# Full-width FFN2 for the first four row tiles of a retention and ELU-MLP kernel, with the second weight matrix loaded by FFN1 tile

## The chip, the cores and the metric

One core of one Trainium2 chip. The metric is device time in microseconds (us) of one execution; a lower number is better. Engines in the profile: PE is TensorE's matmuls, PEld its weight loads, DVE is VectorE, ACT ScalarE, POOL GpSimd, SP SyncE. A "q" after the name is the engine's sequencer, which issues DMAs.

## The reference

```python
# q, k, v: (8, 8, 576, 64), each 0.1 * randn;  w_in: (512, 2048);  w_out: (2048, 512)
scores = q @ k.transpose(0, 1, 3, 2) / sqrt(64)
Dmat   = where(rel >= 0, gamma[h] ** rel, 0)         # rel = query row - key row, causal decay
attn   = (scores * Dmat) @ v                          # (8, 8, 576, 64)
x      = attn.transpose(0, 2, 1, 3).reshape(4608, 512)
h      = x @ w_in                                     # FFN1
g      = where(h > 0, h, exp(min(h, 0)) - 1)          # ELU
out    = g @ w_out                                    # FFN2, (4608, 512) float32
```

## The kernel before

The 4608 rows are 36 units of 128. For each unit: transposes of queries and keys, scores, mask, products, a gating that writes x transposed; then, for groups of units, FFN1 (16 tiles of 128 columns of w_in, each with ELU on ScalarE, GpSimd and VectorE) and FFN2. The order of instructions on every engine is the order of the program. From unit 4 on, everything is interleaved. What concerns us is the start: group 0 is units 0 to 2, group 1 is unit 3; their FFN1 runs while the weights are still coming in, and their FFN2 runs in one piece before the interleaving begins.

```python
def load_w_out(c, f0, f1):                            # by column halves, 256 of 512
    s = (slice(None), slice(f0, f1), slice(c * 256, c * 256 + 256))
    nc.gpsimd.dma_start(w_out_sb[s], w_out_v[s])

def ffn2_cols(u, c0, c1, bank, copy, queue):
    g, it = group_of[u]
    pool, tag = bank
    pm = pool.tile([P, c1 - c0], FP32, name="pmh", tag=tag)
    for ft in range(NFT):                             # 16 matmuls of 256 columns
        nc.tensor.matmul(
            pm, gts[g, ft][:, it * P : (it + 1) * P], w_out_sb[:, ft, c0:c1],
            start=(ft == 0), stop=(ft == NFT - 1),
        )
    ot = opool.tile([P, c1 - c0], FP32, name="oth", tag="ot")
    copy(ot, pm)                                      # VectorE for even u, ScalarE for odd u
    queue.dma_start(out[u * P : (u + 1) * P, c0:c1], ot)
# ...
def load_v(u, after=None, queue=nc.sync):
    vv = raw.tile([P, H, D], FP32, name="rv", tag="rv")
    if after is not None:
        after.memset(vv[0:1, 0, 0:1], 0.0)            # the load waits for this write: a release
    for p0, b, s0, n in place(u):
        queue.dma_start(vv[p0 : p0 + n], v[b, :, s0 : s0 + n, :].rearrange("h p d -> p h d"))
# ... the loads, in this order on GpSimd's queue:
    load_w_in(0)  # after units 1 and 2's queries and keys
    scale_v(0); load_w_in(1); scale_v(1); load_w_in(2)
    load_qk(3); load_v(3, queue=nc.gpsimd); scale_v(2); load_w_in(3)
    load_w_out(0, 0, 16); load_w_out(1, 0, 16)
# ... FFN1 of group 0: tile n needs quarter n // 4 of w_in; unit 3's attention lies within
    for n in range(4, 16):
        f1(0, n, m if n % 4 == 1 else None)
        if n == 9:
            turn(3)
        # ... scale_v(3) in halves at 9 and 10, scores(3) at 11, product(3) at 13
# ... then FFN1 of group 1, and:
    load_qk(4); finish(); load_qk(5); load_v(5, nc.vector); scale_v(4)
    nc.gpsimd.tensor_copy(gx[:, :, S:], gx[:, :, 0:64])
    for u, bank in enumerate((h, h, h, m)):
        ffn2_half(u, 0, bank)                         # all first halves
    load_qk(6); load_v(6, nc.vector); scale_v(5)
    ffn2_half(0, 1, h)                                # second halves between unit 4's attention
    turn(4)
    # ... ffn2_half(1, 1, h), scores(4), ffn2_half(2, 1, h), product(4), turn(5), ffn2_half(3, 1, m)
    f1(2, 0)                                          # FFN1 of unit 4
```

## Time and profile before

| | before |
|---|---|
| time, median of 3 runs | 315.29 us (314.77 to 315.34) |
| span of the profiled run | 313.2 us |
| TensorE busy from 16 to 311 us | 292.73 of 295 us |
| first FFN2 matmul to unit 4's first FFN1 matmul | 32.77 to 49.36, 16.59 us |
| landing of the last quarter of w_in | 25.62 us |
| landing of w_out's two halves | 31.0 and 37.2 us |

TensorE is the bound from 16 us to the end, so a change counts where it alters when TensorE starts, how long its stream is, or where the stream must wait. The lines that show it stand in the prediction. Two reading aids: consecutive matmuls overlap, so their cost is the distance between starts, not their length; and a "landing" here is a DMA's issue plus its time to landing from the DMA view.

### The profile page before, as it was taken

The page shows a single profiled execution, that of the slowest core. Times are in us where ns is not written, and L with a number is a line of the kernel's source. Part 1 is how long each engine was busy: PE and PEld are TensorE (multiplying, and loading weights), DVE is VectorE, ACT ScalarE, POOL GpSimd, SP SyncE. Part 2 cuts the span into 40 slices and gives each one's busy share as a digit, 9 for nine tenths or more (in the row PEclk, how much of TensorE's full clock was granted, in tenths as well). Part 3 has the DMA queues.
Part 4 walks back from the last instruction along what each step waited for, and adds up shares of the span by engine and source line. Part 5 has one row for each costly group of instructions (what it writes and reads, how often), then busy time and mean ns, then how long its engine had stood idle before and what let it go on. Part 6 is the DMA issues. An engine that isn't in the chain of part 4 may idle for free.

```text
span 313.2 us, 7555 instructions
## 1 busy us (share of the span) xinstructions
PE 305.2 (97%) x3028; PEld 173.6 (55%) x3028; DVE 172.5 (55%) x279; ACT 130.8 (42%) x243; POOL 200.2 (64%) x288
## 2 busy tenths in 40 slices
PE   7799999999999999999999999999999999999995
PEld 3477988777765555554554444444444444444444
DVE  4668435756756667655565655565555555434300
ACT  6356215355344543444444443443444344344311
POOL 7977894968977777797777666766664423333300
PEclk9999999999999999999999999999999999999999
DMA  9999999997999999999999999998996200001111
GB/s 156 186 206 199 206 211 177 191 143 75 126 122 178 144 126 195 133 107 198 97 160 134 125 126 132 133 137 128 134 133 86 69 33 36 35 33 39 64 68 68
DMA packets 149219, 39.55 MB, mean 126 GB/s; under 512 B 137600, under 2 KB 145152, under 8 KB 149184
## 3 DMA queue, kind: packets, MB, share of 16 engines
q0 software_dynamic: 79248, 13.64, 56.2%
q1 hardware_dynamic: 67920, 23.14, 39.3%
q10 hardware_dynamic: 2016, 2.29, 2.4%
q8 instruction: 23, 0.38, 0.5%
q14 instruction: 12, 0.10, 0.1%
HBM read 36.70 MB, written 9.44 MB: 147 GB/s over the span
## 4 chain that ended last, share of the span: by engine, by line
PE 88%; DMA 5%; DVE 2%; POOL 2%; SPq 0%; issue 0%; ACT 0%; DVEq 0%; POOLq 0%
PE ph L353 37%; PE pm L378 34%; PE pmh L394 6%; PE sc L212 4%; DMA w_in_sb<-in_moe_w_in_dram 3%; PE o L274 3%; PE st L257 2%; PE o L240 2%; DMA rv<-in_v_dram 2%; PE tr L196 1%; POOL vn L177 1%; DVE pt L224 1%; DVE g L320 1%; POOL qkn L94 1%; POOL w_in_sb L105 0%; DVE xt L287 0%
## 5 line engine op out<-in xcount | busy, mean ns | idle before, releaser
L360 POOL TENSOR_SCALAR m<-e 128x512 bf16<-128x512 f32 (+1 forms) x156 | 90.7, 583 | 95.1 <-ACT e L358 91.5
L353 PE MATMUL ph<-xt,w_in_sb 128*128 128x512 bf16 (+3 forms) x808 | 142.0, 313 | 0.7 <-DVE g L320 0.2
L320 DVE SCALAR_TENSOR_TENSOR g<-ph,m 128x512 bf16<-128x512 f32 (+1 forms) x156 | 99.4, 647 | 76.1 <-POOL m L360 75.3
L358 ACT ACTIVATE e<-ph 128x512 f32<-128x512 f32 (+1 forms) x156 | 87.5, 564 | 124.9 <-PE ph L353 122.1
L378 PE MATMUL pm<-w_out_sb,g 128*128 128x512 bf16 x496 | 125.6, 379 | 0.0
L353 PEld LDWEIGHTS <-w_in_sb 128*128 128x128 bf16 x808 | 68.9, 98 | 53.6 <-DVE g L320 0.9
L378 PEld LDWEIGHTS <-g 128*128 128x128 bf16 x496 | 47.8, 98 | 53.2 <-issue 0.3
L224 DVE TENSOR_TENSOR pt<-sc,mask 128x1024 bf16<-128x1024 f32 (+1 forms) x37 | 44.1, 1193 | 19.7 <-PE sc L212 19.4
L177 POOL TENSOR_TENSOR vn<-rv,gk 128x512 bf16<-128x512 f32 (+1 forms) x37 | 37.8, 1022 | 1.0 <-DMA rv<-in_v_dram 1.0
L94 POOL DMA_DIRECT2D qkn<-in_q_dram x39 | 35.0, 899 | 0.0
L94 POOL DMA_DIRECT2D qkn<-in_k_dram x39 | 33.4, 858 | 0.1
L287 DVE TENSOR_TENSOR xt<-o,gx 128x512 bf16<-128x512 f32 x36 | 24.7, 685 | 14.1 <-PE o L274 13.9
L385 ACT COPY ot<-pm 128x512 f32<-128x512 f32 x31 | 18.1, 585 | 14.5 <-PE pm L378 14.1
L266 ACT CAST sb<-st 128x256 bf16<-128x256 f32 x32 | 11.9, 372 | 19.4 <-PE st L257 16.6
L394 PE MATMUL pmh<-w_out_sb,g 128*128 128x256 bf16 (+1 forms) x176 | 18.3, 263 | 0.0
L394 PEld LDWEIGHTS <-g 128*128 128x128 bf16 x176 | 15.8, 98 | 1.9
L212 PEld LDWEIGHTS <-qkT 64*64 64x64 bf16 x576 | 9.2, 106 | 13.5 <-issue 11.0
L212 PE MATMUL sc<-qkT 64*64 64x128 bf16 x576 | 15.0, 222 | 0.3 <-ACT qkT L198 0.2
L274 PE MATMUL o<-pt,vn 128*64 128x128 bf16 x288 | 14.3, 221 | 0.0
L399 DVE COPY oth<-pmh 128x256 f32<-128x256 f32 (+1 forms) x6 | 2.4, 402 | 18.0 <-PE pmh L394 18.0
L240 PE MATMUL o<-qkT,sb 64*64 64x128 bf16 (+1 forms) x256 | 12.3, 214 | 0.0
L257 PE MATMUL st<-vn,qkn 128*64 128x64 bf16 (+1 forms) x256 | 10.4, 201 | 0.0
(41 smaller groups left out, 89.8 us busy)
## 6 DMA issues: line engine op xcount, KB each, us to landing
rv<-in_v_dram SPq DMA_DIRECT2D x31, 256.0 KB, 5.3
out_dram<-ot SPq DMA_DIRECT2D x27, 256.0 KB, 2.4
qkn<-in_q_dram POOLq DMA_DIRECT2D x31, 128.0 KB, 5.4
qkn<-in_k_dram POOLq DMA_DIRECT2D x31, 128.0 KB, 5.4
w_in_sb<-in_moe_w_in_dram POOLq DMA_DIRECT2D x4, 512.0 KB, 10.0
w_out_sb<-in_moe_w_out_dram POOLq DMA_DIRECT2D x2, 1024.0 KB, 18.0
out_dram<-oth ACTq DMA_DIRECT2D x9, 128.0 KB, 4.7
rv<-in_v_dram SPq DMA_DIRECT2D x8, 128.0 KB, 5.8
```

The lines of the kernel that those rows point to most:

```text
L94: nc.gpsimd.dma_start(kns[u][p0 : p0 + n, c], (q, k)[c][b, :, s0 : s0 + n, :].rearrange("h p d -> p h d"))
L177: nc.gpsimd.tensor_tensor(vns[u][:, h0:h1], raws[u][:, h0:h1], gk[:, u % R, h0:h1].unsqueeze(2).to_broadcast([P, h1 - h0, D]), ALU.mult,)
L212: nc.tensor.matmul(sc[j * 64 : (j + 1) * 64, i, hp], t[r, 1, hp, j * 64 : (j + 1) * 64], t[r, 0, hp], start=(hp == 0), stop=(hp == HP - 1) ...
L224: nc.vector.tensor_tensor(pts[u][:, s].rearrange("p i h t -> p (i h) t"), scs[u][:, s].rearrange("p i h t -> p (i h) t"), m.unsqueeze(1).t ...
L274: nc.tensor.matmul(o[i * D : (i + 1) * D, hp], vns[u][:, h], pts[u][:, i, hp], start=(u % R == 0 and hp == 0), stop=(hp == HP - 1), skip_g ...
L287: nc.vector.tensor_tensor(xts[g][:, :, i * P : (i + 1) * P], os_[u], gx[:, :, s0 : s0 + P], ALU.mult)
L320: nc.vector.scalar_tensor_tensor(gt_, ph, 0.0, m, ALU.max, ALU.min)
L353: nc.tensor.matmul(ph[:, i * n : (i + 1) * n], w_in_sb[:, j, f : f + P], xts[g][:, j, :n], start=(j == 0), stop=(j == KJ - 1), skip_group_ ...
L358: nc.scalar.activation(e[:, w], ph[:, w], AF.Exp)
L360: nc.gpsimd.tensor_scalar(m[:, w], e[:, w], -1.0, 1.0, ALU.add, ALU.mult)
L378: nc.tensor.matmul(pm, gts[g, ft][:, it * P : (it + 1) * P], w_out_sb[:, ft], start=(ft == 0), stop=(ft == NFT - 1))
L394: nc.tensor.matmul(pm, gts[g, ft][:, it * P : (it + 1) * P], w_out_sb[:, ft, c0:c1], start=(ft == 0), stop=(ft == NFT - 1),)
```

## The change

The intent: each FFN2 matmul of the first four units covers all 512 columns, in four banks held open at once, first with FFN1 tiles 0 to 7 of all four units, so that only the first half of w_out's rows is needed at first; hence w_out comes in two parts by FFN1 tile. Unit 3's values leave GpSimd's busy queue.

```diff
-    def load_w_out(c, f0, f1):
-        s = (slice(None), slice(f0, f1), slice(c * 256, c * 256 + 256))
-        nc.gpsimd.dma_start(w_out_sb[s], w_out_v[s])
+    def load_w_out(f0, f1):
+        nc.gpsimd.dma_start(w_out_sb[:, f0:f1], w_out_v[:, f0:f1])
...
-    def ffn2_half(u, c, bank):
-        ffn2_cols(u, c * 256, c * 256 + 256, bank, A if u % 2 else V, nc.scalar)
+    def ffn2_part(u, f0, f1, bank):
+        g, it = group_of[u]
+        if f0 == 0:
+            pool, tag = bank
+            acc[u] = pool.tile([P, DM], FP32, name="pm", tag=tag)
+        for ft in range(f0, f1):
+            nc.tensor.matmul(
+                acc[u], gts[g, ft][:, it * P : (it + 1) * P], w_out_sb[:, ft], start=(ft == 0), stop=(ft == NFT - 1)
+            )
+        if f1 == NFT:
+            ot = opool.tile([P, DM], FP32, name="ot", tag="ot")
+            (A if u % 2 else V)(ot, acc[u])
+            nc.scalar.dma_start(out[u * P : (u + 1) * P, :], ot)
...
     load_qk(3)
-    load_v(3, queue=nc.gpsimd)
     scale_v(2)
     load_w_in(3)
-    load_w_out(0, 0, 16)
-    load_w_out(1, 0, 16)
+    load_w_out(0, 8)
+    load_w_out(8, 16)
...
         product(u)
+        if u == 1:
+            load_v(3, nc.vector)
...
     for u, bank in enumerate((h, h, h, m)):
-        ffn2_half(u, 0, bank)
+        ffn2_part(u, 0, 8, bank)
     load_qk(6)
     load_v(6, nc.vector)
     scale_v(5)
-    ffn2_half(0, 1, h)
+    ffn2_part(0, 8, 16, None)
     turn(4)
... (units 1 to 3 alike)
```

More of the change, by code (lines that the diff above doesn't have):

```diff
@@ L374, in ffn2 @@
             pool, tag = ((ps_o, "o"), (ps_m, "pm"), (ps_h, "ph"))[it] if g == NG - 1 else (ps_m, "pm")
-            acc[0] = pool.tile([P, DM], FP32, name="pm", tag=tag)
-        pm = acc[0]
+            acc["pm"] = pool.tile([P, DM], FP32, name="pm", tag=tag)
+        pm = acc["pm"]
         for ft in range(part * 4, part * 4 + 4):
@@ L503 @@
     load_v(7, nc.vector)
-    ffn2_half(1, 1, h)
+    ffn2_part(1, 8, 16, None)
     scores(4)
@@ L507 @@
     scale_v(6)
-    ffn2_half(2, 1, h)
+    ffn2_part(2, 8, 16, None)
     product(4)
@@ L512 @@
     load_v(8, nc.vector)
-    ffn2_half(3, 1, m)
+    ffn2_part(3, 8, 16, None)
     scores(5)
```

## The prediction

> **What bounds the kernel now.** I read the page's first two parts, then the busy time of the engines by stretch, then the chain that ended last around the changed stage, then the instructions in order of time there, and last the DMA issues one by one.
>
> From the page, parts 1 and 2 and the ends of parts 3 and 5 (busy shares; tenths of busy time in 40 slices of 7.8 us; two groups):
>
> ```profile
> PE 305.2 (97%) x3028; PEld 173.6 (55%) x3028; DVE 172.5 (55%) x279; ACT 130.8 (42%) x243; POOL 200.2 (64%) x288
> ...
> PE   7799999999999999999999999999999999999995
> ...
> PEclk9999999999999999999999999999999999999999
> DMA  9999999997999999999999999998996200001111
> ...
> L378 PE MATMUL pm<-w_out_sb,g 128*128 128x512 bf16 x496 | 125.6, 379 | 0.0
> ...
> L394 PE MATMUL pmh<-w_out_sb,g 128*128 128x256 bf16 (+1 forms) x176 | 18.3, 263 | 0.0
> ```
>
> TensorE is full from slice 3 on, at full clock, and no other engine is above 64%. A mean of 379 ns is the length of one matmul with its drain; it is not what it costs, because 496 of them have a union of only 125.6 us. The cost is the spacing from start to start. The views by stretch confirm the bound (columns: stretch, length, busy, count, clock, DMA share, GB/s; first TensorE alone, then all matmuls of the half-width FFN2 line):
>
> ```profile
> 16.00:311.00 295.00, 292.73 (x2889) 1.00 0.97 124
> ...
> 32.77:41.50 8.73, 8.72 (x80) 7.73 (x80) 1.00 1.60 195
> ```
>
> From 16 to 311 us TensorE lacks 2.3 us of 295. The second line is the changed stage: 80 half-width matmuls in 8.73 us are 109.1 ns each. In full width the same page's rows of four in the chain take 0.86 us, so 0.2157 us each: two halves cost 0.2182, one whole 0.2157.
>
> The chain of waits in order of time from 12 to 52 us (start, length, what):
>
> ```profile
> 12.82 0.89 POOL rv L85
> 13.71 0.98 POOL vn L177
> 14.69 10.93 DMA w_in_sb<-in_moe_w_in_dram
> 25.62 0.05 issue
> 25.67 1.47 PE ph L353 x8
> ...
> 32.94 8.73 PE pmh L394 x80
> 41.67 0.45 PE tr L196 x8
> 42.12 1.75 PE pmh L394 x16
> 43.86 0.35 PE sc L212 x16
> 44.21 1.85 PE pmh L394 x16
> ```
>
> The reader is to see that the chain enters TensorE only once, where the last quarter of w_in lands at 25.62 us, and then stays there. That entry looks like 11 us behind GpSimd's work (unit 3's values issued at 12.82 stand in it), but TensorE had work of its own until 25.6: the start of 25.67 is only some 0.13 us later than the spacing after the scores would have it (spacing between these starts 0.275 us more than the usual one, and 0.145 of that is what every change from scores back to full-array matmuls shows, as at 44.15 and 49.36). So at most 0.13 us hang on that load. Neither half of w_out appears: the first was issued at 15.50 and landed 15.5 us later, at 31.0, used from 32.77; the second issued at 16.64, landing after 20.5 us, at 37.2, used from about 39.75 (32.77 plus 64 times 0.109).
>
> The stage where the tightest hand-over lies, in order of time (start, length, engine, line, count; in brackets idle before):
>
> ```profile
> 41.51 0.61 PE L196 MATMUL tr<-ident,qkn 128*128 128x128 bf16 x8
> 41.71 0.42 DVE L399 COPY oth<-pmh 128x256 f32<-128x256 f32 x1 [3.07 <-PE pmh L394]
> ...
> 42.16 0.42 DVE L197 COPY qkT<-tr 128x512 bf16<-128x512 bf16 x1
> ...
> 42.85 0.58 ACT L198 COPY qkT<-tr 128x512 bf16<-128x512 bf16 x1 [2.52 <-DVE rv L83]
> ...
> 43.80 0.42 PE L212 MATMUL sc<-qkT 64*64 64x128 bf16 x16
> ```
>
> The last piece of unit 4's keys is issued at 36.35 and takes 5.2 us (the DMA view of that moment), so it lands at about 41.5: as the transposes start, whose key half runs 0.22 us in. And ScalarE's copy of the transposed half ends at 43.43, 0.37 us ahead of the scores that read it.
>
> **What the Trainium skill says.** "TensorE: Matmul & The Clock Gate", section Back-to-back issue gap: a warm matmul is spaced N/2.4 + 2.5 ns. The trace agrees: 109.1 against 109.2 for N = 256, 215.7 against 215.8 for N = 512. Halving the number of matmuls saves only the fixed 2.5 ns. Weight loads overlap here (98 ns each, under the 109 ns of a half), so having fewer is worth nothing more.
> "DMA: Bandwidth & Descriptors", section Issuing engines are not separate DMA queues: all queues share the same 16 DMA engines, and another issuer saves only issue time. The trace agrees in that DMA is at 9 tenths throughout this part.
> The same page, section Why small descriptors are slow (HBM only): a fixed cost per packet, worth attention at 256 B or less. The w_out parts go from 1 KB to 2 KB pieces of source (512 B to 1 KB written), so little is to be had: in the stretch 13 to 18 us (w_in, 1 KB pieces written) the core moves 206 GB/s, in 26 to 30 us (w_out, 512 B) 199, 3% less.
>
> **The change part by part.**
> 1. FFN2 at full width: 128 matmuls at 109.1 ns (13.96 us) become 64 at 215.7 (13.81). On the path: -0.16 us.
> 2. Copies out of PSUM: eight of 128x256 (0.42 us on VectorE, 0.37 on ScalarE) become four of 128x512, an estimate of 0.67 and measured 0.585 (the page's 128x512 copy on ScalarE). Less work in total (3.2 to 2.5 us), but each single one is 0.2 us longer, and unit 0's stands ahead of the transposes' copies. Old order: 0.42 copy from 41.71, then qkT on VectorE, then qkT on ScalarE, slack some hundredths to a few tenths. New: the last part ends some 0.1 us earlier, the copy starts at about 41.6 and ends at 42.27, qkT on VectorE ends near 42.7, ScalarE near 43.5; scores want to start at about 43.7. Estimate 0 to +0.15 us, mean +0.05. At unit 2's copy the new end of about 46.75 just meets unit 4's gating at 46.89: 0.
> 3. Banks: all four accumulators stay open from 32.77 to 49. Nobody else takes these banks meanwhile (transposes and scores use another pair, the products two others), and the next FFN1 tiles take those of units 0, 1 and 2, copied out 5 us and more before for the first two and 2 us for the third. The first use of each of the four banks falls where it did (8 times 0.2157 is 1.73 us per unit, 16 times 0.1091 is 1.75). 0.
> 4. w_out by FFN1 tile: the first part is needed at 32.77 as before, the second at 32.77 + 32 times 0.2157 = 39.67 rather than 39.75. Landings at about 31 and 37, or 0.2 to 0.6 us earlier if the 3% of rate holds over 10.9 us of transfer. No wait before, none after: 0 directly. What it gives is that unit 4's keys, which queue behind it, start earlier.
> 5. Unit 3's values from GpSimd's queue to SyncE: GpSimd issues w_in's last quarter 0.92 us earlier (the issue took 0.92). But the queue is backed up: that quarter waits 10.9 us from issue to landing, behind 512 KB of w_in, unit 3's queries and keys and the values themselves. The values held the queue from the keys' landing (11.93 + 10.5 = 22.4) to their own (12.79 + 10.5 = 23.3), 0.87 us. On SyncE they move as 1,024 pieces of 256 B; the unit loads at the start of the trace pass some 935 such pieces a microsecond, so 1.1 us of all engines, taken from the same transfers. Balance: between -0.2 and +0.2 us on a landing that holds TensorE by 0.13. Estimate 0, between -0.13 and +0.25. They themselves land at 22 to 23, needed on GpSimd at 24.65.
> 6. A part not in the intent: the VectorE write that releases unit 6's values comes in program order behind the copies of the first halves (38.58 us). Those copies are gone, so it comes right after unit 5's (35.00): 256 KB more in small pieces compete with unit 4's keys, while 256 KB of output writes leave that stretch. At a share of half the pieces after 38.5 us I make this +0.4 us on the keys' landing, from which the earlier w_out (0.2 to 0.6) and the missing writes are to be taken. TensorE wants the keys 0.1 us earlier than before. Estimate 0 to +0.5, mean +0.1.
>
> Sum: -0.16 + 0.05 + 0 + 0 + 0 + 0.1 = about 0. Tail and middle (50 to 313 us) are untouched, and TensorE carries any shift of the start through to the end one for one.
>
> **The rivals.** (a) Keys late: part 6 wins, and TensorE stands before unit 4's transposes by up to 1 us: 316.2. For it: the landing and the use coincide at 41.5. Against: w_out earlier. (b) The issue order on GpSimd really holds the start: then the whole 0.92 us would come off, 314.2. For it: the chain names that issue. Against: 10.9 us from issue to landing of 512 KB is queueing, and TensorE waited only 0.13. (c) The longer copies or the four held banks hold the scores or the next FFN1 tiles, +0.2 to +0.5 us: 315.7. Against: the slacks above. (d) The values on SyncE starve behind the w_in flood (unit 4's took 7.0 us in the same state from its issue at 30.53) and land after 24.65; GpSimd then runs late in FFN1: +0.5.
>
> **Range and chances.** 315.2 us, the old median within the noise of its three runs (314.77 to 315.34). Low 314.4: parts 1 and 5 at their best and some of (b). High 316.2: rival (a). A 2% change would be 6.3 us; nothing in this stage holds so much, as TensorE had only 2.3 us of idle time to give in the whole span, and no wait of mine exceeds 1 us. Faster 0.01, same 0.98, slower 0.01.
>
> **What would show it.** Right: 64 full-width matmuls spaced 215.7 ns from about 32.7; w_out never named as a wait; w_in's last quarter landing within 0.3 us of 25.6; TensorE's idle time in the stretch of 33 to 50 us under 0.5 us. Wrong: a wait of TensorE on unit 4's keys near 41.4 of over 0.5 us, on GpSimd's values or FFN1 tiles near 27, on the copied qkT near 43.7; or the first FFN1 matmul after the load of w_in starting near 24.8, which would be rival (b) and would need TensorE's earlier work to have moved as well.

## The result

315.77 us median of 6 runs (315.10 to 316.76) against 315.20 of before in the same rounds (314.77 to 315.47): ratio 1.0022, 95% interval 1.0002 to 1.0043. A ratio is the mean time of one kernel's runs over that of the other's of the same rounds, so not quite the ratio of the medians quoted. On another chip (run a1_again below) the same kernel gave 1.000. So: the same within 2%, perhaps 0.1 to 0.2% slower, and within the predicted range.

The profile of the changed kernel, its page (parts 1 and 3, then the new FFN2 line):

```profile
PE 303.1 (96%) x2925; PEld 167.5 (53%) x2964; DVE 172.1 (55%) x278; ACT 130.4 (41%) x241; POOL 199.3 (63%) x287
...
q0 software_dynamic: 77120, 13.37, 54.6%
q1 hardware_dynamic: 68960, 23.40, 38.6%
...
L408 PE MATMUL pm<-w_out_sb,g 128*128 128x512 bf16 x61 | 14.2, 379 | 0.2
```

PEld fell by 64 weight loads (3028 to 2964), as it should when 128 matmuls become 64. The FFN2 line has only 61 of its 64 records: matmul records are missing from this trace, and wherever one is missing the spacing shows 0.43 us in place of 0.216. That, and not a wait, is the idle "0.2". Queue q0 is GpSimd's, q1 SyncE's. Before, they had 79,248 and 67,920 packets. q1 gained 1,040 and q0 lost 2,128. w_out in rows of twice the length saves 2,048 of the latter; the values of unit 3 account for the other 80. So the same 256 KB went as some 64 packets of 4 KB on GpSimd's queue and go as 1,024 of 256 B on SyncE's (the remaining 16 each are the completion marks).

The chain of waits, which answers to the one shown of before (start, length, what):

```profile
14.98 12.83 DMA w_in_sb<-in_moe_w_in_dram
27.81 0.05 issue
27.86 1.47 PE ph L352 x8
...
35.39 8.37 PE pm L408 x38
43.76 0.45 PE tr L195 x8
...
45.93 0.35 PE sc L211 x16
```

The shape is the same: one entry by the last quarter of w_in, then TensorE only. But the entry is at 27.81 rather than 25.62. And TensorE's waits from 14 to 53 us (before had neither; its only one there, of 0.2 us at 52.88, comes just after 53 in the changed kernel):

```profile
PE ph L334 <- DMA w_in_sb<-in_moe_w_in_dram: 1.1, 1, 1.1
PE ph L352 <- DMA w_in_sb<-in_moe_w_in_dram: 0.5, 1, 0.5
```

The first is at the very first FFN1 matmul, which waited for the first quarter of w_in. That quarter was issued at 5.68 us and landed at 17.39; before, at 5.67 and 15.43. The first difference between the two programs is the issue of unit 3's values, at 12.8 us of before. So these 2 us are no effect of the change that the program can show, but scatter in the first loads. The second is the change's business, at least in part.

Comparing the two traces mark by mark gives the whole account of their 1.48 us:

| stretch | before | after | difference |
|---|---|---|---|
| start to first FFN1 matmul | 15.87 | 17.43 | +1.56 |
| to FFN1 tile 12, the first that needs the last quarter of w_in | 9.80 | 10.43 | +0.63 |
| to first FFN2 matmul | 7.10 | 7.10 | 0.00 |
| FFN2 stretch, to unit 4's first FFN1 matmul | 16.59 | 16.42 | -0.17 |
| to the last scores (unit 35) | 209.09 | 209.09 | 0.00 |
| to the end | 54.74 | 54.20 | -0.54 |

From 51 to 260 us the two streams are the same to 0.01 us. The last row is not scatter, although no edit aims at it. TensorE's last work and the issue of the last write fall at the same distance from the last scores in both; what differs comes after that issue (before, span 313.2, then changed, span 314.7):

```profile
310.16 0.33 SPq L400 DMA_DIRECT2D out_dram<-oth  x1
```

```profile
312.18 0.33 SPq L399 DMA_DIRECT2D out_dram<-oth  x1
```

From there to the end of the span it is 3.03 and 2.49 us. All nine traces with full-width FFN2 have 2.5 to 2.6, all five with half width 3.0. The instruction records show where it goes: at the end of the program SyncE passes a fixed list of waits for semaphores, 0.06 us each. Before, the wait for the last write is followed by five others; in the changed kernel it is the last of the list (0.3 us). Another 0.2 us is VectorE's closing instruction, which ends later in before. So 0.3 of the 0.5 us come of another semaphore standing for the last write. This is read from the two traces; no run tests it by itself.

### The profile page after: what moved, and what is told of

The parts are those of the page before. It is cut to its first block, busy times and chain, and to the rows that moved or that the text cites. A ratio compares the mean times of both kernels' runs of the same rounds, so it can differ in the third digit from the quotient of the medians.

```text
span 314.7 us, 7377 instructions
## 1 busy us (share of the span) xinstructions
PE 303.1 (96%) x2925; PEld 167.5 (53%) x2964; DVE 172.1 (55%) x278; ACT 130.4 (41%) x241; POOL 199.3 (63%) x287
## 4 chain that ended last, share of the span: by engine, by line
PE 87%; DMA 7%; DVE 2%; POOL 1%; issue 1%; SPq 1%; ACT 0%; DVEq 0%
PE ph L352 37%; PE pm L377 33%; PE pm L408 4%; DMA w_in_sb<-in_moe_w_in_dram 4%; PE sc L211 4%; PE o L273 3%; DMA rv<-in_v_dram 2%; PE st L256 2%; PE o L239 2%; PE tr L195 1%; PE pmh L393 1%; DVE pt L223 1%; DVE g L319 1%; POOL vn L176 1%; POOL qkn L94 1%
## 5 line engine op out<-in xcount | busy, mean ns | idle before, releaser
L377 PE MATMUL pm<-w_out_sb,g 128*128 128x512 bf16 x478 | 122.8, 379 | 1.6 <-issue 1.0
L377 PEld LDWEIGHTS <-g 128*128 128x128 bf16 x496 | 47.8, 98 | 53.2 <-issue 0.3
L265 ACT CAST sb<-st 128x256 bf16<-128x256 f32 x32 | 11.9, 372 | 20.2 <-PE st L256 17.4
L408 PE MATMUL pm<-w_out_sb,g 128*128 128x512 bf16 x61 | 14.2, 379 | 0.2
L197 ACT COPY qkT<-tr 128x512 bf16<-128x512 bf16 x12 | 7.0, 584 | 15.4 <-DVE rv L83 9.5
L422 PE MATMUL dum<-warm 128*128 128x512 bf16 x26 | 8.9, 480 | 1.2 <-DVE warm L119 1.2
```

Of the source, the lines that this page charges most:

```text
L377: nc.tensor.matmul(pm, gts[g, ft][:, it * P : (it + 1) * P], w_out_sb[:, ft], start=(ft == 0), stop=(ft == NFT - 1))
L408: nc.tensor.matmul(acc[u], gts[g, ft][:, it * P : (it + 1) * P], w_out_sb[:, ft], start=(ft == 0), stop=(ft == NFT - 1))
```

## The experiments

The twelve kernels ran in three batches of four (a; b0, b3, c1, d1; c2, e1, b5, b4). Each was timed against the kernel before on the same chip in the same rounds (six runs each, five of e1, four of b5 and b4), and the four of one batch share those runs of before. Since starts scatter by more than the effects, the verdicts rest on stretches between marks in the traces, one trace for each run. The table leaves out b5 and b4, which have waits of their own. All twelve runs gave correct results.

| trace | unit 3's values by | first FFN1 | w_in: last quarter lands after first | FFN1 to tile 12 | unit 6's values issued after FFN2's start | unit 4's last keys land after FFN2's start | FFN2 stretch |
|---|---|---|---|---|---|---|---|
| before | GpSimd | 15.87 | 10.19 | 9.80 | 5.92 | 8.73 | 16.59 |
| b0_before | GpSimd | 15.49 | 10.33 | 10.00 | 5.92 | 8.95 | 16.63 |
| after | SyncE | 17.43 | 10.42 | 10.43 | 2.82 | 8.36 | 16.42 |
| a1_again | SyncE | 16.27 | 10.97 | 10.55 | 2.80 | 9.32 | 17.02 |
| a2_values_only | SyncE | 17.12 | 10.97 | 9.67 | 5.92 | 8.42 | 16.58 |
| a3_wide_only | GpSimd | 15.67 | 10.26 | 9.88 | 2.83 | 9.48 | 17.10 |
| a4_two_halves | SyncE | 15.22 | 11.82 | 11.24 | 2.82 | 9.39 | 17.15 |
| b3_late_v6 | SyncE | 15.67 | 11.40 | 10.98 | 7.53 | 6.89 | 16.42 |
| c1_wide_late_v6 | GpSimd | 15.66 | 11.11 | 10.77 | 7.54 | 6.98 | 16.42 |
| c2 (c1 again) | GpSimd | 16.33 | 10.52 | 10.88 | 7.53 | 6.87 | 16.42 |
| d1_before_early_v6 | GpSimd | 15.76 | 11.18 | 10.78 | 2.83 | 9.18 | 16.86 |
| e1_w_in_split | GpSimd | 15.72 | 10.16 | 9.66 | 7.53 | 7.73 | 16.42 |

### a1_again: the changed kernel, unedited

> The changed kernel once more, unedited, to see whether its 0.2% loss is there on another chip. Theory 1 (the time is the landing of the last quarter of w_in plus a fixed path on TensorE; the values on SyncE delay that landing by some 0.2 us, the full width saves 0.16, and the rest of the difference between the two profiles is the luck of the first loads): ratio 1.000 to 1.002, so at most +0.6 us; the stretch from the first FFN2 matmul to the first FFN1 matmul of unit 4's group again 16.4 us (before 16.6), and the landing of w_in's last quarter 10.3 to 10.6 us after that of its first (before 10.2). Theory 2 (all of it is luck of the first loads): ratio 0.999 to 1.001. Theory 3 (the change itself makes the first loads slower, although no instruction ahead of 12.8 us differs): the first quarter of w_in lands near 17.4 us again rather than at 15.4, and the ratio is 1.004 or more.

Measured: 315.74 us (315.13 to 316.39), before 315.98 (314.93 to 316.56), ratio 1.000 (0.998 to 1.002). The first quarter of w_in landed at 15.80, so theory 3 falls: the late start of the first trace was luck. But the stretch that I expected at 16.4 was 17.02, a miss. In order of time around unit 4's transposes, and VectorE's releases just before:

```profile
42.56 0.39 PE L195 MATMUL tr<-ident,qkn 128*128 128x128 bf16 x4
43.38 0.38 PE L195 MATMUL tr<-ident,qkn 128*128 128x128 bf16 x4 [0.44 <-DMA qkn<-in_k_dram]
```

```profile
36.15 0.06 DVE L83 MEMSET rv<- 1x1 f32 x2
42.76 0.69 DVE L413 COPY ot<-pm 128x512 f32<-128x512 f32 x1 [6.55 <-PE pm L408]
```

The eight transposes are split in two: the second four, of the keys, begin 0.82 us after the first in place of 0.22. Idle is put at 0.44 because the modelled end of the first four is subtracted; by spacing the wait is 0.60 us. It is on the last piece of unit 4's keys, which landed at 43.25. And two releases stand together at 36.15: unit 5's values and unit 6's. This is rival (a) of the prediction.

### a2_values_only: only the move of unit 3's values, in the kernel before

```diff
     load_qk(3)
-    load_v(3, queue=nc.gpsimd)
     scale_v(2)
...
         product(u)
+        if u == 1:
+            load_v(3, nc.vector)
```

> Only the move of unit 3's values to SyncE, in the kernel before. Theory 1: the last quarter of w_in lands 10.3 to 10.6 us after the first instead of 10.2; time +0.1 to +0.6 us over before; FFN2 stretch 16.6 us as before. Theory 2: time within 0.1 us of before. The issue-bound rival (GpSimd's issue order holds the start): the last quarter lands 0.5 to 0.9 us earlier and the time falls by as much.

Measured: 316.00 us against 315.98, ratio 1.0008 (0.9991 to 1.0025). The last quarter landed 10.97 us after the first, in the expected range, and the issue-bound rival is refuted: nothing came earlier. FFN2 stretch 16.58, no wait. But tile 12 came only 9.67 us after the first FFN1 matmul, because that one started late in this trace (17.12, with the first quarter landed at 15.52): the granted clock was 0.81 from 8 to 17 us here, so TensorE reached FFN1 late by itself and the late quarter was hidden behind that. So the move delays the load, and whether TensorE feels it depends on the start.

### a3_wide_only: the change without the move

```diff
     load_qk(3)
+    load_v(3, queue=nc.gpsimd)
     scale_v(2)
...
-        if u == 1:
-            load_v(3, nc.vector)
```

> The change without the move of unit 3's values: full width, four banks, w_out by FFN1 tile, values on GpSimd's queue as before. Theory 1: FFN2 stretch 16.4 us, last quarter of w_in 10.2 us after the first, time 0.1 to 0.3 us below before (ratio 0.999 to 1.000). Theory 2: the same within noise. The rival that the held banks and longer copies cost: FFN2 stretch 16.7 us or more, time above before.

Measured: 315.80 against 315.98, ratio 1.0001 (0.9982 to 1.0020). The last quarter 10.26 us after the first, as expected with the values back on GpSimd's queue. The FFN2 stretch was 17.10, not 16.4: again the keys, 0.67 us by spacing. The rival that I had named for 16.7 or more, held banks and longer copies, is not what it is: the wait is on a DMA. The time, expected 0.1 to 0.3 us below before, shows no difference.

### a4_two_halves: the full-width matmuls split in two again

```diff
         for ft in range(f0, f1):
-            nc.tensor.matmul(acc[u], gts[...], w_out_sb[:, ft], start=(ft == 0), stop=(ft == NFT - 1))
+            for c in (0, 256):
+                nc.tensor.matmul(
+                    acc[u][:, c : c + 256], gts[...], w_out_sb[:, ft, c : c + 256],
+                    start=(ft == 0 and c == 0), stop=(ft == NFT - 1), skip_group_check=True,
+                )
```

> The changed kernel with each full-width FFN2 matmul of the first four units split into two of 256 columns into the same bank; order, loads and copies are unchanged. Theory 1: the FFN2 stretch goes from 16.4 to 16.6 us (64 times 2.5 ns), the time rises by 0.15 us over the changed kernel. If weight loads of the halves were in the way, as a rival has it, the stretch would be 17 us or more.

Measured: 315.80 us, ratio to before 1.0010 (0.9988 to 1.0031). The stretch was 17.15 us with a wait for the keys of 0.57; without it 16.58. That is 0.16 us over the 16.42 that the undisturbed wide traces have, as expected for 64 fixed costs of 2.5 ns.

### b0_before: the kernel before, unedited

> The kernel before, unedited, for a second trace of it: how far its start varies by itself. Expected: ratio 0.999 to 1.001. If the luck of the first loads is in both kernels (theory 1), its first quarter of w_in lands anywhere from 14.6 to 17.4 us as in the traces so far, but the last quarter 10.2 us after the first within 0.2, and the stretch from the first FFN2 matmul to the first FFN1 matmul of unit 4 is 16.58 us with no wait at unit 4's transposes.

Measured: 315.21 us, ratio 0.9996 (0.9976 to 1.0017); 10.33 us between the quarters; FFN2 stretch 16.63, with unit 4's keys landing 8.95 us into it and costing 0.04 us by spacing. So the hand-over that the prediction called the tightest does in fact touch in the old kernel. Runs of before range from 314.77 to 316.78 us: the scatter is the old kernel's too. Part of it goes with the clock: in each of the three batches two of the eleven runs of before had a mean clock of 0.995, and they were 0.6 to 1.1 us longer on average than the other nine.

### b3_late_v6: the changed kernel with unit 6's values released later

```diff
+    load_v(6, nc.gpsimd)
     load_qk(6)
-    load_v(6, nc.vector)
     scale_v(5)
```

> The changed kernel with unit 6's values released by a write on GpSimd after its copy of gx (near 40.2 us if FFN2 starts at 32.8) instead of by the write on VectorE that now comes near 35. Theory A (unit 6's early values delay the last piece of unit 4's keys, and TensorE waits for it half way through unit 4's transposes: 0.57 to 0.67 us in three traces): the wait is gone, the FFN2 stretch is 16.42 us. Rival (the keys are late because four output writes were bunched or because w_out's second part lands with them): the wait of some 0.6 us remains and the stretch is 17.0.

Measured: 315.71 us against 315.26, ratio 1.0012 (0.9991 to 1.0033). The transposes are whole again, and unit 4's keys landed 6.89 us into the stretch rather than 9.3 to 9.5:

```profile
42.39 0.61 PE L195 MATMUL tr<-ident,qkn 128*128 128x128 bf16 x8
```

FFN2 stretch 16.42 us. Theory A holds; the rival falls. The time is not better than before's. The values of unit 3 are still on SyncE, and in this trace unit 3's keys were late, so that its transposes waited 0.53 us by spacing, and the last quarter of w_in came 11.40 us after the first.

### c1_wide_late_v6 and c2_wide_late_v6_again: both causes taken away

The changed kernel with the edits of a3 and b3 together.

> Candidate for better than both: full width, four banks and w_out by FFN1 tile, but unit 3's values left on GpSimd's queue and unit 6's values released on GpSimd near 40.2 us. By theory 1 and theory A together: last quarter of w_in 10.2 us after the first, FFN2 stretch 16.42 us, so 0.17 us faster than before at an equal start, 0.2 to 0.6 faster than the changed kernel; ratio to before 0.998 to 1.000, hardly clear of the noise.

> The candidate once more, unedited, beside the next one. If its gain is real: ratio to before 0.998 to 0.9995, FFN2 stretch 16.42 us. If its first result was luck of the starts: ratio within 0.9995 to 1.001.

Measured: 315.02 us (314.97 to 315.17) against 315.26, ratio 0.9987 (0.9969 to 1.0005); and again 315.28 (314.29 to 316.46) against 315.65, ratio 0.9990 (0.9969 to 1.0011). FFN2 stretch 16.42 both times. The direction is as expected; the size stays inside the noise. With the 0.5 us at the end it should have been some 0.7 us at an equal start; the waits that follow took part of it back. An expectation missed in c1: the last quarter of w_in came 11.11 us after the first rather than 10.2, and TensorE waited 1.0 us for it, though the values were on GpSimd's queue. d1 has the same (11.18). In both, the quarter landed 3.3 us after unit 3's values; in the other traces with that queue it was 2.3 to 2.5. What took the extra 0.9 us isn't shown. A 16 KB packet of the instruction queue, of 0.94 us, falls near 24.3 us in these traces, but in those without the delay too. In c2 the wait was elsewhere: TensorE waited 1.0 us for the scaled values of unit 2, whose load landed only at 17.58.

### d1_before_early_v6: the kernel before with that release moved early

```diff
     load_v(5, nc.vector)
+    load_v(6, nc.vector)
     scale_v(4)
...
     load_qk(6)
-    load_v(6, nc.vector)
```

> The kernel before with one edit: the write on VectorE that releases unit 6's values comes right after that of unit 5 (near 35 us) rather than behind the copies of the first halves (38.6). Theory A: the last piece of unit 4's keys lands 0.4 to 0.8 us later against the start of the FFN2 stretch, TensorE waits 0.4 to 0.8 us within unit 4's transposes, FFN2 stretch 17.0 to 17.3 us, time +0.4 to +0.7. Rival: stretch 16.6 as before.

Measured: 316.00 against 315.26, ratio 1.0021 (1.0003 to 1.0039). The wait at the same place appears in the old kernel: 0.27 us by spacing, stretch 16.86, keys landing 9.18 us in rather than 8.73 and 8.95.

```profile
42.38 0.89 PE L196 MATMUL tr<-ident,qkn 128*128 128x128 bf16 x8
```

The eight transposes take 0.89 us in place of the 0.61 that they take undisturbed. The direction is right, the size was overestimated: I had expected 0.4 to 0.8. In the wide kernel TensorE comes to the transposes 0.10 us earlier (40 times 0.2157 is 8.63 us, 80 times 0.1091 is 8.73), which makes 0.37 of it comparable with 0.6; the other 0.2 goes with the landing, which is 0.1 to 0.3 us earlier than the 9.3 to 9.5 of the wide traces. Why it is earlier isn't shown. Most of the 0.2% in time is not from this, though: the profiled run waited 1.0 us for w_in.

### b5_wide_column_halves and b4_tiles_half_width: each half of the change alone

b5 is the changed kernel with the old w_out loads, b4 the old kernel with the new ones.

> The changed kernel with w_out loaded by column halves as before, so the loads of the change undone under its matmuls. Each full-width matmul needs both halves, and the second lands near 37.2 us when FFN2 could start at 32.8: a wait of TensorE of some 4.4 us on w_out at the first FFN2 matmul, time +3.5 to +4.5 us (ratio 1.011 to 1.014). If the loads had no part in it, as one might think from their never having shown as a wait: no change.

> The kernel before with w_out loaded by FFN1 tile and nothing else: the halves of 256 columns want tile 8 after 8 matmuls, 0.87 us into the stage, when the second part lands near 36.5 to 37.2 us: a wait of 2.9 to 3.6 us, FFN2 stretch 19.5 to 20.2 us, time +2.5 to +3.6 us (ratio 1.008 to 1.011).

Measured: b5 322.09 us (319.31 to 323.90) against 315.65, ratio 1.020 (1.016 to 1.024), so unclear whether it passes 2%; b4 318.43 us (317.13 to 319.82), ratio 1.008 (1.005 to 1.011). TensorE's longest wait in b5, then in b4:

```profile
PE pm L409 <- DMA w_out_sb<-in_moe_w_out_dram: 3.8, 1, 3.8
```

```profile
PE pmh L393 <- DMA w_out_sb<-in_moe_w_out_dram: 2.7, 1, 2.7
```

By spacing they are 4.0 and 2.9 us, as expected from the landings. So the load that never showed as a wait is a condition: order of use and order of arrival had to change together. b5's median is 6.4 us above before's, more than its wait and more than the 3.5 to 4.5 expected; b4's is 2.8 us above, but its runs fall in two pairs, 1.5 and 1.9 us above at a mean clock of 1.000, 3.7 and 4.2 us above at 0.992 and 0.994. b4's trace, one of the second pair, shows what the lower clock costs (stretch, length, busy and count of PE and PEld at the FFN2 line, granted clock, DMA share, GB/s):

```profile
36.80:41.10 4.30, 4.29 (x25) 3.21 (x25) 0.60 1.65 169
```

In the 4.3 us after the wait TensorE was granted 0.60 of its clock on average. The first eight matmuls still kept the usual spacing; then 15 of 256 columns were spaced 0.213 us, twice the usual, which cost 1.7 us more; the FFN2 stretch came to 21.1 rather than the 19.5 to 20.2 that I had expected. For b5 the profiled run kept its clock (1.000, span 317.5), and its three other runs had mean clocks of 0.984 to 0.989 and spans of 319.7 to 322.1. That the lower clock is what sets them apart fits (1.1% of 318 us is 3.5), but those runs have no trace.

### e1_w_in_split: the candidate with the last quarter of w_in in two pieces

```diff
-    def load_w_in(n):
-        s = slice(n * 512, (n + 1) * 512)
+    def load_w_in(n, a=0, b=512):
+        s = slice(n * 512 + a, n * 512 + b)
...
     load_qk(3)
+    load_w_in(3, 0, 256)
     load_v(3, queue=nc.gpsimd)
     scale_v(2)
-    load_w_in(3)
+    load_w_in(3, 256, 512)
```

> The candidate with the last quarter of w_in loaded in two pieces of two FFN1 tiles, the first ahead of unit 3's values, the second behind them. If TensorE's one remaining wait in this part, at FFN1 tile 12, is for that load (0.13 us in the first trace of before, 0.28 to 0.9 us in others): the wait is gone, tile 12 starts straight after unit 3's scores, 0.1 to 0.8 us earlier against the first FFN1 matmul, and the time is 0.1 to 0.6 us below the candidate's. If it only moves the wait to tile 14 or to unit 3's values on GpSimd, nothing is gained.

Measured: 314.25 us (314.11 to 314.25, 5 runs) against 315.65, ratio 0.9956 (0.9941 to 0.9972): the one version whose interval lies clear below before, by some 1.4 us (0.4%). The first piece landed at 23.53, the second at 25.49, unit 3's values at 24.43. Tile 12 came 9.66 us after the first FFN1 matmul, the shortest of all traces, beside a2's 9.67 with its late start. TensorE in order of time at that place:

```profile
25.03 0.42 PE L211 MATMUL sc<-qkT 64*64 64x128 bf16 x16
25.38 1.47 PE L352 MATMUL ph<-xt,w_in_sb 128*128 128x384 bf16 x8
```

The distance of 0.35 us between scores and FFN1 is the bare one; before had 0.48 (25.19 to 25.67), and in b0_before it was 0.68. The chain of waits of this trace between 20 and 36 us is TensorE alone. From the first FFN1 matmul to that of unit 4 it took 33.21 us, against 33.49 and 33.73 in the two traces of before and 33.95 and 34.68 in those of the changed kernel. That accounts for 0.3 to 0.5 us of the 1.4 against before, and the end of the program, which e1 has in common with all wide versions, for another 0.5. Of the rest, 0.1 us is that none of its five runs had the clock of 0.995 that two of before's eleven had; what remains is good starts, which may be luck, as the six runs of c2 beside it scatter by 2.2 us.

## Why the prediction was right

The time and the verdict were right (315.2 predicted, 315.77 and 315.74 measured, range 314.4 to 316.2). Its own signs were mixed: the spacing of 215.7 ns came, and w_out never showed as a wait; but w_in's last quarter landed at 27.81 and 26.77 us rather than within 0.3 of 25.6, and in a1_again TensorE stood 0.60 us before unit 4's keys, which the prediction names as a sign of being wrong. Its steps:

- **Part 1, width.** Predicted -0.16 us. Shown: 16.42 us in six traces of the wide kernel without another wait, 16.58 to 16.63 in three of the narrow one, and 16.58 when a4's wait is taken off. The skill's N/2.4 + 2.5 ns holds to 0.1 ns.
- **Part 2, copies.** Predicted mean +0.05. In the changed kernel's trace VectorE's copy of 512 columns took 0.69 us, the ScalarE copy of qkT ended at 45.53 and the scores started at 45.86 after only the usual change of array mode. No wait: 0.
- **Part 3, banks.** Predicted 0, and 0 it is: no trace has a wait of FFN2 or of the next FFN1 on a bank beyond the 0.2 us that before had.
- **Part 4, w_out.** No wait, as predicted. The rate rose by 4% (28.5 to 32.5 us, w_out in both: 199 GB/s before, 207 after), and the second part landed 10.2 to 11.1 us after w_in's last quarter in the eight traces with the new loads (e1, of another order, left out), 11.0 to 11.8 in the five with the old ones: 0.6 us earlier on average, as said, with the ranges touching. What the prediction did not say, and b5 shows, is that the full width without this part would have waited 4.0 us for w_out; b4 shows that the new loads without the full width wait 2.9.
- **Part 5, unit 3's values.** Predicted 0, between -0.13 and +0.25. This term was too small. The last quarter of w_in landed 10.4 to 11.8 us after the first in six traces with the values on SyncE (mean 11.16, b5 with 11.37 included), 10.2 to 11.2 in seven with GpSimd (mean 10.56, b4 with 10.35 included): +0.6 us, with overlap. e1, whose order is another, is left out. Unit 3's keys show it without overlap: 7.8 to 9.2 us after the first quarter against 7.0 to 7.3. The working, 1,024 small packets at 1.1 us against 0.87 us of the same bytes in large ones, is right as to the packets (the queue counts show 64 against 1,024), but its rate of 935 a microsecond fits only if all packets are counted: of the 7,756 up to 10 us, 3,027 were on GpSimd's queue, which has pieces of 128 B there. Of 256 B packets some 810 a microsecond passed between 1.8 and 5 us, where they were nearly alone, so an estimate of 1.3 us rather than 1.1. That covers part of the +0.6. No run separates the size of the packets from the other queue and the later release, and TensorE's own loss is less sure than the landing's: in a2, the only run of this part alone, TensorE was late already and lost nothing, and c1 and d1, with the values on GpSimd's queue, waited as long as any.
- **Part 6, unit 6's values.** This is the term most mis-sized: predicted 0 to +0.5, mean +0.1; measured 0.60, 0.67 and 0.57 in three of four traces of kernels with this early release, and 0 in the first, where w_out's second part landed earliest (3.2 us after FFN2's start against 3.7 to 4.0 in the others). The mechanism was right, and rival (a) is real: with the release 2.8 us into the stretch the keys landed at 9.2 to 9.5 (8.4 in that first trace), at 5.9 us 8.4 to 9.0, at 7.5 us 6.9 to 7.7, where the keys' transposes start at 8.9 if nothing delays them. The prediction set the missing output writes and the earlier w_out against it; together they did not cover it.
- **The end.** The prediction called everything after 50 us untouched. That is wrong by -0.5 us, in all nine wide traces (see The result).
- **The sum.** Parts 5 and 6 cost more than part 1 saves; a3 and b3 show part 6, a2 the delay of part 5. That the total was nevertheless near 0 is luck: the end, which the prediction did not foresee, gave back 0.5. Counted from the first FFN1 matmul, the two traces of the changed kernel end 0.1 us earlier and 0.6 us later than the first trace of before. The prediction also assumed that the start repeats within the scatter of three runs (0.6 us); it doesn't: over all versions the first FFN1 matmul lies between 15.2 and 17.4 us, and runs of before alone reach from 314.77 to 316.78.
- **Rival (b)**, GpSimd's issue order, is refuted by a2 and a3. **Rival (c)**, held banks, too. **Rival (d)** half: the values did crawl (15.26 to 24.03, 8.8 us, in the changed kernel), and in a2 they landed at 26.37, but no trace shows TensorE waiting for them.

What stays open: what makes the first loads differ by 2 us from run to run; the extra 0.9 us of w_in's last quarter in c1 and d1; what in part 5 costs, the small packets or the moment and the queue; why d1's keys came earlier than the wide kernel's.

## What to carry to other kernels

Merging two matmuls of 256 columns that share a weight saves 2.5 ns each when weight loads are hidden: look for waits, not for widths. When a copy is removed from an in-order engine, everything behind it moves forward, the releases of loads too (here from 5.9 to 2.8 us after FFN2's start); ask what these loads will collide with, and release a load behind the transfer that is needed first. And a queue that is full for 20 us should be ordered by first use at the size of first use: cutting one load in two so that its urgent half passes another took away a wait that was 0.13 to 1.1 us in eleven of the other traces. Last, when a program's time moves by half a microsecond, look at its end too: here the closing waits and what follows them made 0.5 us, three times what the wider matmuls saved.

## What the Trainium skill lacked or had wrong

- "TensorE: Matmul & The Clock Gate", Back-to-back issue gap: it gives about 131 ns per matmul of 512 columns as the sustained spacing in a stream of weight loads and matmuls. Here, with a weight load for each, it is 215.7 ns throughout (40 in 8.63 us). That is the formula of the same section that the prediction used, of which the page says that it holds for an isolated matmul and is too high for a stream.
- The same page, HAM oscillation, warns of TensorE gaps of over 3.4 us for the clock. Here a wait of 2.9 us by spacing (2.7 by the profile) was followed by a lower one: 0.60 on average over the next 4.3 us in b4. And one of 4.0 us in b5's profiled run was not (1.000). These are one trace each, and a2's has a lower clock too (0.81 from 8 to 17 us) after waits of 1.2 us at most, so that the wait of 2.9 us brought it about isn't shown.
- "DMA: Bandwidth & Descriptors", Issuing engines are not separate DMA queues: it says that the issuing engine only saves issue time. Here it also set the packets: 256 KB in rows of 256 B made some 64 packets on GpSimd's queue, which agrees with the packets of preferably at most 4096 B that the same page describes under SWDGE vs HWDGE vs iDMA, and 1,024 on SyncE's. On its own queue beside the weights the load took 8.8 us from issue to landing, and unit 3's keys came 0.5 to 2.2 us later for it (7.8 to 9.2 against 7.0 to 7.3). The section says nothing of that.
- No page gives the time of a change of TensorE between full-array and 64-row matmuls; it would belong to "TensorEngine Tiling (Array Packing)". In all fourteen traces the scores start 0.094 us later than the usual spacing after a full-array matmul (203 against 109 ns, 310 against 216), and the first full-array matmul after them starts 0.148 us after the last of the scores, which themselves start in fours, one four every 0.056 us.
